# Linear attention and a gated two-layer network: three plain and three large token blocks in place of two and four

## The chip, the cores and the metric

The kernel runs on one core of a Trainium2 chip. TensorE (PE) multiplies 128x128 tiles into PSUM banks; VectorE (DVE), ScalarE (ACT) and GpSimd (POOL) work on tiles in SBUF and PSUM; SyncE (SP) and the other engines issue transfers to and from DRAM. Each engine runs its own instructions in order and waits on semaphores of the others. The metric is the device time of one execution in microseconds (us), and lower is better. Before the change it is 928.02 us, the median of three runs (927.49 to 928.74).

## The reference

There are 8 batches of 576 tokens, with 8 heads of 64. Linear attention is followed by two matrix products with a gate between them:

```python
q_s = softmax(q, axis=-1)            # over the 64 numbers of a head
k_s = softmax(k, axis=2)             # over the 576 tokens of a batch
kv  = einsum('bhsd,bhse->bhde', k_s, v)
x   = einsum('bhsd,bhde->bhse', q_s, kv)   # heads side by side: 4608 x 512
h   = x @ w_in                       # 512 -> 2048
g   = h * clip(h + 3, 0, 6) / 6
out = g @ w_out                      # 2048 -> 512
```

Everything is float32, and the two weight matrices come as 64-bit floats, as raw words.

## The kernel before, in words

**Precision.** A float32 operand is split into a high part `hi` (an ACT cast to fp32r) and a rest `lo` (a DVE subtraction), and each product is three matmuls: hi by hi, hi by lo, lo by hi. `split` (L122 to L124) does that for weights, for x and for g.

**Token blocks.** The 4608 tokens are taken in blocks. The first two are plain blocks of 512. For each of the 16 chunks `f` of 128 hidden numbers, `gemm1` (12 matmuls of 512 columns into a bank `ph`), the gate `relu6` and a split of g into a tile `gp`, then `gemm2` (12 matmuls into four banks `po`). In block 0 a chunk's weights are also decoded from raw words on DVE and ACT (`decode`, L130 to L156, two chunks ahead). Block 0's `gemm2` comes two chunks behind its `gemm1`, block 1's one chunk behind.

The other four are large blocks of 896 tokens. Each product is done by a seven-product scheme on 2x2 blocks (a form of Strassen's), so that seven block products replace eight. `phase1` does the first product of a large block, 56 steps of 6 matmuls of 448 columns, `phase2` the second. The seven combinations of x (`factors`, tiles `right0` to `right6`) and those of g are made on DVE and ACT. The weights' combinations are the same for all large blocks. They are made once and put into two DRAM buffers `kept` (in the profile `wf`), and `fetch` reads them back into tiles `left`, two steps' worth of 512 KB at a time, five groups deep.

**The weights' combinations.** Per pair of chunks and per side (w_in, w_out), three of the seven are plain blocks, written by `plain_weights` from the split weights in SBUF. The other four are sums, made by `sum_weights`: it rebuilds the float32 blocks as hi + lo, with an ACT copy of hi (L430) and an accumulating transfer of lo that POOL issues (L431); then come four DVE passes (L434 to L437), two splits into the chunks' own places, and four transfers to `kept`. Thirteen of the sixteen sums are made in plain block 1. Three (`late_sums`) are made in the first large block's `phase1`, from blocks already in DRAM (L425 and L426, from `kept` and `spare`).

**Attention** is done per pair of heads. For plain blocks it is `attention` (softmax of k and q, nine TensorE transposes, `pkv`, `px`). For large ones it is `sb_attention`: the query softmax `q_softmax_t` runs on transposed tiles, with four POOL copies `swap` for each of its two reductions, a POOL copy `kb` for the k maximum, and a DVE stream transpose into one tile `m`; then come `pm`, `pkv` and `px`. The work is cut into steps, and the loop over chunks advances them: a step or two of the next block's attention per chunk.

**Places.** The decoded weights live in two pools of chunk places (`EARLY`: chunks 0 to 9, then 10 to 15). When the plain blocks are through with a pool, `next_stage` closes it and opens the large blocks' operand tiles there. The PSUM has eight banks, two for attention and six for `ph`, `po` and the large products `x`, `y`, `z`. The ring `v` of three tiles is shared by decode, sums and outputs, `gp` has three.

**What sets the order.** The kernel is written once, and a scheduler that works with planned times sets each engine's order; from plain block 1 on TensorE keeps the program's order. So work written into one block can stand in the one before it, on any of the other engines.

Of the kernel before, what the change touches and what calls it, by code (L numbers as in the profile page):

```python
# [22 lines left out]
TH = 448  # L23
# [9 lines left out]
def attention_moe(  # L33
# [58 lines left out]
    def flip(out, in_):  # L92
# [12 lines left out]
    EARLY = 10  # L105
    stages = [ExitStack(), ExitStack()]
    wp = [
        stage.enter_context(tc.tile_pool(name=f"w{i}", bufs=1, side=side, reuse_waits="tile"))
        for i, (stage, side) in enumerate(zip(stages, ("right", "left")))
    ]  # L110

    def place(f, dt, name):
        return wp[f >= EARLY].tile([P, 4 * DM], dt, name=name, tag=f"w{f}")

# [5 lines left out]
    wi, wo, raws = {}, {}, {}  # L120

# [8 lines left out]
    def decode(f):  # L130
# [17 lines left out]
        nc.vector.tensor_tensor(vu, vu, low, op=ALU.add)  # L148
        parts = place(f, F32R, f"w_{f}").rearrange("p (s i n) -> p s i n", s=2, i=2)
# [39 lines left out]
    def kv_of(j, hp, ke, vt):  # L189
# [9 lines left out]
        kv = att.tile([P, P], F32, name="kv", bufs=8)  # L199
# [50 lines left out]
    def attention(j, hp):  # L250
# [3 lines left out]
        else:  # L254
            kt, ke, vt = load_k(j, hp)
            qt = att.tile([P, TB], F32, name="qt", bufs=2)
# [5 lines left out]
        q_softmax(qt, j == 1, nc.vector if j else nc.gpsimd)  # L262
# [69 lines left out]
    def sb_attention(s, hp):  # L332
        t0 = START + s * SB
        need = [b for b in range(t0 // S, (t0 + SB - 1) // S + 1)]
        qt = att.tile([P, SB], F32, name="qt", bufs=2)
        nc.sync.dma_start(qt, qf[s, hp])
        loads = {b: load_k(b, hp, tokens=True) for b in need if (b, hp) not in kvs}
        new = {}
# [19 lines left out]
        yield  # L358
# [27 lines left out]
    late_sums = [(7, 0), (6, 1), (7, 1)]  # L386
    kept = [dr.tile([P, NSLOT, TB], F32, name=f"wf{i}") for i in range(2)]

    spare = dr.tile([P, len(late_sums), TB], F32, name="spare")

    def keep(pair, side, block, src):
        to = kept[side][:, SLOT[side][pair, PRODUCT[block]]]
        nc.sync.dma_start(to, src)

    def halves(pair, side):

        a, b = (wi, wo)[side][2 * pair], (wi, wo)[side][2 * pair + 1]
        one, two = a[:, :, 0:HT], a[:, :, HT:]
        if side:
            return one, b[:, :, 0:HT], b[:, :, HT:], two  # L400
        return one, two, b[:, :, HT:], b[:, :, 0:HT]

    def plain_weights(pair, side):
        for block, src in zip((A11, A12, A22, None), halves(pair, side)):
            if block is not None:
                to = kept[side][:, SLOT[side][pair, PRODUCT[block]]]
            elif (pair, side) in late_sums:
                to = spare[:, late_sums.index((pair, side))]
            else:
                continue  # L410
# [318 lines left out]
    def steps(units):  # L729
        for unit in units:  # L730
            for _ in unit:
                yield
# [139 lines left out]
```

## Time and profile before

| | |
|---|---|
| median of three runs | 928.02 us (927.49 to 928.74) |
| the profiled execution's own time | 925.28 us |
| its span, first to last instruction | 923.5 us |
| PE busy | 841.9 us (91%), 4328 matmuls |
| DVE busy | 711.8 us (77%) |
| ACT busy | 486.6 us (53%) |
| POOL busy | 141.0 us (15%) |
| DRAM read and written | 174.75 and 39.58 MB |

Busy times are shares of the whole span and average stages that differ: weights are decoded in block 0, sums made in block 1, and only products and attention are left later. In the timeline `x48` after a row means 48 instructions merged into it, and a bracket gives the idle time before the row and what ended it. Most matmuls go through one helper and carry line L87, most splits L123 and L124, so rows are told apart by their tiles.

### The profile page before, as it was taken

Reading aid. Unit: us, or ns where it says so; the run is one execution under the profiler, and the core shown is the slowest. Engines: PE = TensorE matmul, PEld = TensorE weight load, DVE = VectorE, ACT = ScalarE, POOL = GpSimd, SP = SyncE. Lnnn points to the kernel's source line nnn. Section 1 sums busy time; section 2 is a strip of 40 time slices with the busy share of each in tenths; the row PEclk is TensorE's granted clock in tenths of the full one; section 3 lists DMA queues with packets and bytes.
Section 4 is the critical chain, followed back from the end, with each engine's and each line's share of the span. In section 5 each row is a group of like instructions: output and inputs, shape, how many; then the busy total and the mean of one; then the engine's idle time right before and its main releaser. Section 6 shows DMA issues by size and latency. Waiting matters only on the chain.

```text
span 923.5 us, 12980 instructions
## 1 busy us (share of the span) xinstructions
PE 841.9 (91%) x4328; PEld 722.7 (78%) x4328; DVE 711.8 (77%) x1193; ACT 486.6 (53%) x858; POOL 141.0 (15%) x242
## 2 busy tenths in 40 slices
PE   4699986979975888999999999899999999999998
PEld 3478764858763677897898888699889979998997
DVE  7999997478878468989848979984867794555873
ACT  7897642445554345556445555644545644444553
POOL 4112232344543321101101100110100000000000
PEclk9889996999987798999999999999999999999999
DMA  9994545898997896875788887577756668666674
GB/s 371 413 395 162 171 138 163 207 258 231 269 280 245 234 346 222 300 225 178 235 275 287 274 300 227 180 242 253 248 189 188 203 199 265 223 210 206 214 237 154
DMA packets 90291, 222.02 MB, mean 240 GB/s; under 512 B 9072, under 2 KB 35952, under 8 KB 88176
## 3 DMA queue, kind: packets, MB, share of 16 engines
q1 hardware_dynamic: 80432, 211.75, 68.7%
q0 software_dynamic: 9216, 8.39, 5.9%
q10 hardware_dynamic: 576, 1.05, 0.3%
q8 instruction: 35, 0.57, 0.3%
q14 instruction: 32, 0.26, 0.1%
HBM read 174.75 MB, written 39.58 MB: 232 GB/s over the span
## 4 chain that ended last, share of the span: by engine, by line
PE 52%; DVE 23%; issue 9%; DMA 9%; POOL 4%; ACT 2%; SPq 0%; DVEq 0%; ACTq 0%; POOLq 0%
PE x L87 28%; PE y L87 11%; PE z L87 9%; DMA v<-w 3%; POOL v L431 2%; PE px L87 2%; DVE gf L124 2%; DVE v L144 2%; DMA kt<-in_kT_dram 2%; DVE right L124 2%; DVE v L148 2%; DVE g L522 2%; DVE w L124 1%; DMA v<-spare 1%; DVE gp L124 1%
## 5 line engine op out<-in xcount | busy, mean ns | idle before, releaser
L87 PE MATMUL x<-right,left 128*128 128x448 f32 x768 | 178.4, 380 | 16.3 <-DVE g L561 11.7
L123 ACT CAST gf<-g 128x448 fp32r<-128x448 f32 x224 | 126.7, 567 | 125.7 <-PE x L87 57.0
L87 PEld LDWEIGHTS x<-right,left 128*128 128x128 f32 x768 | 146.7, 193 | 33.4 <-DVE g L561 13.0
L87 PE MATMUL x<-gf,left 128*128 128x448 f32 x768 | 163.9, 369 | 4.8 <-DVE gf L124 4.5
L124 DVE TENSOR_TENSOR gf<-g,gf 128x448 fp32r<-128x448 f32 x224 | 135.8, 618 | 38.6 <-ACT gf L123 37.1
L87 PEld LDWEIGHTS x<-gf,left 128*128 128x128 f32 x768 | 144.5, 189 | 20.9 <-DVE gf L124 9.1
L87 PE MATMUL po<-w,gp 128*128 128x512 f32 x384 | 104.4, 422 | 6.4 <-DVE gp L124 3.6
L87 PE MATMUL ph<-x,w 128*128 128x512 f32 x384 | 100.0, 408 | 2.3 <-DVE x L124 1.5
L521 ACT ACTIVATE r<-g,three 128x896 f32<-128x896 f32 (+1 forms) x64 | 54.9, 857 | 83.2 <-DVE g L565 42.2
L87 PEld LDWEIGHTS po<-w,gp 128*128 128x128 f32 x384 | 76.2, 203 | 25.3 <-DVE gp L124 5.1
L87 PEld LDWEIGHTS ph<-x,w 128*128 128x128 f32 x384 | 73.9, 195 | 22.4 <-ACT x L123 2.0
L87 PE MATMUL z<-gf,left 128*128 128x448 f32 x384 | 83.2, 372 | 5.8 <-DVE gf L124 5.5
L87 PE MATMUL y<-right,left 128*128 128x448 f32 x384 | 87.5, 374 | 0.0
L87 PEld LDWEIGHTS z<-gf,left 128*128 128x128 f32 x384 | 72.5, 191 | 15.2 <-DVE gf L124 9.5
L87 PEld LDWEIGHTS y<-right,left 128*128 128x128 f32 x384 | 72.5, 190 | 7.5 <-issue 0.6
L522 DVE SCALAR_TENSOR_TENSOR g<-r,g 128x896 f32<-128x896 f32 (+1 forms) x64 | 54.5, 851 | 9.3 <-ACT r L521 9.3
L431 POOL DMA_DIRECT2D v<-w x52 | 45.7, 1000 | 64.6 <-ACT v L430 28.3
L123 ACT CAST w<-v 128x512 fp32r<-128x512 f32 (+1 forms) x42 | 32.3, 783 | 30.8 <-DVE v L435 21.2
L87 PE MATMUL z<-right,left 128*128 128x448 f32 x192 | 44.8, 368 | 0.0
L304 POOL COPY swap<-qr 32x28 f32<-32x28 f32 x64 | 27.3, 427 | 103.6 <-DVE qr L315 74.8
L565 DVE TENSOR_TENSOR g<-g,y 128x448 f32<-128x448 f32 x32 | 19.7, 617 | 30.1 <-PE y L87 30.1
L87 PE MATMUL px<-m,kv 128*128 128x128 f32 (+6 forms) x112 | 32.3, 436 | 10.8 <-DVE qr L305 10.8
(124 smaller groups left out, 1184.3 us busy)
## 6 DMA issues: line engine op xcount, KB each, us to landing
left<-wf SPq DMA_DIRECT2D x224, 512.0 KB, 4.2
wf<-w SPq DMA_DIRECT2D x100, 256.0 KB, 4.0
raw<-in_w_dram SPq DMA_DIRECT2D x16, 1024.0 KB, 14.0
vt<-in_v_dram SPq DMA_DIRECT2D x28, 325.0 KB, 5.9
kt<-in_kT_dram SPq DMA_DIRECT2D x28, 288.0 KB, 4.9
ke<-in_k_dram SPq DMA_DIRECT2D x24, 320.0 KB, 5.2
qt<-in_qf_dram SPq DMA_DIRECT2D x16, 448.0 KB, 4.2
out_dram<-v SPq DMA_DIRECT2D x16, 448.0 KB, 4.2
```

Of the source, the lines that this page charges most:

```text
L87: nc.tensor.matmul(out, lhsT, rhs, start=start, stop=stop, skip_group_check=goes_on)
L123: nc.scalar.copy(hi, src)
L124: engine.tensor_sub(lo, src, hi.bitcast(F32))
L144: nc.vector.scalar_tensor_tensor(vu, high, 0xC0000000, m, op0=ALU.bitwise_and, op1=ALU.bitwise_or)
L148: nc.vector.tensor_tensor(vu, vu, low, op=ALU.add)
L304: nc.gpsimd.tensor_copy(swap[r : r + QD], stat[o : o + QD])
L431: nc.gpsimd.dma_start(t, src[:, 1].bitcast(F32), accum_op=ALU.add)
L521: nc.scalar.activation(r, h, AF.Relu, bias=three, scale=1.0)
L522: nc.vector.scalar_tensor_tensor(g, r, 6.0, h, op0=ALU.min, op1=ALU.mult)
L565: nc.vector.tensor_add(h21, h21, y)
```

## The change

The block sizes become 3 x 512 and 3 x 1024 tokens. `TH`, half a large block, goes from 448 to 512, so a large product's matmul has 512 columns, and there are three large blocks rather than four. The rest follows:

- Attention for plain block 2 is added (`attention(2, ...)` during block 1), and the first large block's attention is advanced during block 2.
- `decode` also writes the float32 chunk to a DRAM tensor `whole`, for chunks 6 to 15 (`FROM_DRAM = 3` pairs are left out).
- `sum_weights` no longer uses POOL. For the first three pairs it adds hi and lo on DVE (L407), for the others it reads both chunks back from `whole` in one transfer (L410), a step ahead of its use. Its results go to `gp` tiles rather than to the chunks' places. The sixteen sums are spread, a step per chunk, over blocks 1 and 2; none are left for the large blocks.
- There is one pool of chunk places. The `right` tiles use places 0 to 6, the tiles of g places 7 to 14, and of the six `left` groups two use place 15 and four the `gp` ring, which has four tiles. The last plain block takes chunk 15 first.
- `qt` has one buffer rather than two, and an `sb_attention` unit now loads one step before it computes; `px` of a unit comes after the loads of the next. The temporaries of the gate use `g` and `v`.
- The steps that advance the next block's attention and `factors` inside large blocks are at other slots.

```diff
-TH = 448
+TH = 512
...
+    FROM_DRAM = 3
+    whole = dr.tile([P, NFC, 2 * DM], F32, name="whole")
...
+        if f // 2 >= FROM_DRAM:
+            nc.sync.dma_start(whole[:, f], v)
...
-        qt = att.tile([P, SB], F32, name="qt", bufs=2)
+        qt = att.tile([P, SB], F32, name="qt", bufs=1)
         nc.sync.dma_start(qt, qf[s, hp])
         loads = {b: load_k(b, hp, tokens=True) for b in need if (b, hp) not in kvs}
+        yield
...
         w4 = moe.tile([P, 2 * DM], F32, name="v", bufs=3)
-        if late:
-            for n, block in enumerate((A11, A12, A22, None)):
...
-                nc.sync.dma_start(t, src[:, 0:HT])
-                nc.gpsimd.dma_start(t, src[:, HT:], accum_op=ALU.add)
+        if pair < FROM_DRAM:
+            for i in range(2):
+                hi, lo = ((wi, wo)[side][2 * pair + i][:, e].bitcast(F32) for e in (0, 1))
+                nc.vector.tensor_add(w4[:, i * DM : (i + 1) * DM], hi, lo)
         else:
-            for n, src in enumerate(halves(pair, side)):
-                t = w4[:, n * HT : (n + 1) * HT]
-                nc.scalar.copy(t, src[:, 0].bitcast(F32))
-                nc.gpsimd.dma_start(t, src[:, 1].bitcast(F32), accum_op=ALU.add)
+            src = whole[:, 2 * pair : 2 * pair + 2, side * DM : (side + 1) * DM]
+            nc.sync.dma_start(w4.rearrange("p (f n) -> p f n", f=2), src)
+            yield
...
-            if late:
-                dst = moe.tile([P, 2, TB], F32R, name="gp", tag="gp", bufs=3)
-            else:
-                dst = (wi, wo)[side][2 * pair + i]
+            dst = moe.tile([P, 2, TB], F32R, name="gp", bufs=4).rearrange("p i n -> p (i n)")
...
-    GROUP, GROUPS = 2, 5
+    GROUP, GROUPS = 2, 6
...
+    for j in range(NB):
+        if j == 1:
+            in_order.append(True)
+        if j < NB - 1:
+            step = steps([attention(j + 1, hp) for hp in range(NP)], 4)
+        else:
+            step = steps([sb_attention(0, hp) for hp in (0, 2, 1, 3)], 6)
+            fac = factors(0)
+        chunks = [*range(NFC)] if j < NB - 1 else [NFC - 1, *range(NFC - 1)]
+        for n, f in enumerate(chunks):
...
+            if j == 1 and f % 2:
+                plain_weights(f // 2, 0)
+                plain_weights(f // 2, 1)
+            if j:
+                next(sums, None)
...
         def between1(i):
-            if not s and i in (12, 24, 36):
-                sum_weights(*late_sums[i // 12 - 1])
-            if i % 5 in (1, 3):
+            if i % 2:
                 next(step, None)
 
         def between2(i):
-            if i > 16 and i % 2:
+            if i % 2 and i < 16:
                 next(step, None)
-            if i in (31, 33, 35, 37, 39, 41, 43):
+            if i in (18, 21, 33, 36, 39, 42, 45):
                 next(fac, None)
```

How the order of instructions moves is seen at three places. First POOL, in the plain block in which the sums are made. Before, the copies that the large softmax (`swap`) and the k maximum (`kb`) need stand between accumulating transfers:

```order
L304 COPY swap<-qr 32x28 x4
L431 DMA v<-w_309 128x256 x2
L431 DMA v<-w_337 128x256 x2
L431 DMA v<-w_309 128x256
L431 DMA v<-w_337 128x256 x2
L431 DMA v<-w_309 128x256
L431 DMA v<-w_369 128x256 x2
L431 DMA v<-w_425 128x256 x2
L304 COPY swap<-qm 32x28 x2
L343 COPY kb<-km 128x128
```

After the change, from the last split of block 0 on:

```order
L121 TENSOR_TENSOR w_1165<-v,w_1165 128x2x512
L343 COPY kb<-km 128x128
L303 COPY swap<-qm 32x32 x4
L343 COPY kb<-km 128x128
L303 COPY swap<-qr 32x32 x4
L303 COPY swap<-qm 32x32 x4
```

POOL has no transfer left, there or later. Second DVE, at the end of plain block 0, from a chunk's gate (`g<-g,ph`) to the last `kv` that this block's attention makes. Before:

```order
L522 SCALAR_TENSOR_TENSOR g<-g,ph 128x512
L311 TENSOR_REDUCE qm<-qt 128x28
L197 TENSOR_SCALAR rk<-pkv 128x1
L341 TENSOR_REDUCE km<-kt 128x1
L315 TENSOR_REDUCE qr<-qt 128x28
L124 TENSOR_TENSOR gp<-g,gp 128x512
L198 RECIPROCAL rk<-rk 128x1
L200 SCALAR_TENSOR_TENSOR kv<-pkv,rk,mask 128x128
```

After:

```order
L196 TENSOR_SCALAR rk<-pkv 128x1
L121 TENSOR_TENSOR gp<-g,gp 128x512
L219 TENSOR_REDUCE qm<-qt 128x8
L417 TENSOR_TENSOR v<-v 128x256
L197 RECIPROCAL rk<-rk 128x1
L498 SCALAR_TENSOR_TENSOR g<-g,ph 128x512
L419 TENSOR_TENSOR v<-v 128x256
L199 SCALAR_TENSOR_TENSOR kv<-pkv,rk,mask 128x128
```

The passes of the large softmax (`128x28` results) and the large blocks' `km` are gone from here; a plain block's softmax and the first sum (L417, L419) stand in their place. Third DVE again, near the end of the last plain block after the change, where a large block's queries are transposed out of the single `qt` buffer and the next pair's maximum is taken from it:

```order
L320 STREAM_TRANSPOSE m<-qt 128x1024
L121 TENSOR_TENSOR gp<-g,gp 128x512
L498 SCALAR_TENSOR_TENSOR g<-g,ph 128x512
L310 TENSOR_REDUCE qm<-qt 128x32
L121 TENSOR_TENSOR gp<-g,gp 128x512
```

Two rows stand between the transpose and the reduction over the next load of the same buffer. Before the change that reduction read the other buffer.

More of the change, by code (lines that the diff above doesn't have):

```diff
@@ L102, in attention_moe @@
     nc.gpsimd.memset(three, 3.0)
[L105 to L110, printed above, removed]
+    wp = ctx.enter_context(tc.tile_pool(name="wp", bufs=1))
     def place(f, dt, name):
-        return wp[f >= EARLY].tile([P, 4 * DM], dt, name=name, tag=f"w{f}")
+        return wp.tile([P, 4 * DM], dt, name=name, tag=f"w{f}")
     late = iter(range(NFC - 1, -1, -1))
@@ L357, in sb_attention @@
             kv_of(b, hp, ke, vt)
-        yield
         yield
@@ L469, in attention_moe @@
     )
+    turn = iter(range(10**6))
     def fetch(count=1):
@@ L475, in fetch @@
                 return
-            t = operand("left", TB, bufs=GROUPS)
+            at = next(turn) % GROUPS
+            if at > 1:
+                t = moe.tile([P, 2, TB], F32R, name="gp", bufs=4)
+            else:
+                if not ring:
+                    ring.append(place(15, F32R, "left").rearrange("p (r k n) -> p r k n", r=2, k=2))
+                t = ring[0][:, at]
             g = key[2] * GROUP
@@ L727, in attention_moe, with steps @@
     decode(1)
-    def steps(units):
+    def steps(units, length):
+        before = None
         for unit in units:
-            for _ in unit:
+            next(unit)
+            yield
+            if before:
+                next(before, None)
+            for _ in range(length - 2):
+                next(unit)
                 yield
+            before = unit
+        yield
+        next(before, None)
+        yield
     accs = {}
-    done2 = []
     def work(j, n, f, g):
@@ L742, in work, with all_sums @@
             store(j, accs[j])
-        if j and f % 2:
-            plain_weights(f // 2, 1)
-            if (f // 2, 1) not in late_sums:
-                sum_weights(f // 2, 1)
-        if j and f == EARLY - 1:
-            next_stage(0)
-            fetch(GROUPS)
+    def all_sums():
+        for some in (range(FROM_DRAM), range(FROM_DRAM, NPAIR)):
+            for side in range(2):
+                for pair in some:
+                    yield from sum_weights(pair, side)
+    sums = all_sums()
@@ L751, in attention_moe @@
     LAG = 2
     pend = []
-    step = steps([attention(1, hp) for hp in range(NP)])
-    for f in range(NFC):
-        if f + AHEAD < NFC:
-            load_w(f + AHEAD)
-        g = gemm1(0, f)
-        if f + 2 < NFC:
-            decode(f + 2)
-        for _ in range(2 if f % 4 == 3 else 1):
-            next(step, None)
-        pend.append((0, f, f, g))
-        if len(pend) > LAG:
-            work(*pend.pop(0))
-    in_order.append(True)
-    step = steps([sb_attention(0, hp) for hp in (0, 2, 1, 3)])
@@ L782, in attention_moe @@
     for args in pend:
         work(*args)
-    for _ in fac:
+    for _ in sums:
         pass
-    next_stage(1)
+    with tc.high_priority():
+        for _ in fac:
+            pass
+        fetch(GROUPS - 2)
     for s in range(NS):
         more = s + 1 < NS
-        step = steps([sb_attention(s + 1, hp) for hp in (0, 2, 1, 3)]) if more else iter(())
+        step = steps([sb_attention(s + 1, hp) for hp in (0, 2, 1, 3)], 6) if more else iter(())
         fac = factors(s + 1) if more else iter(())
```

104 lines of the change are left out of this document (42 added, 62 removed).

## The prediction

> **What bounds the kernel now.** I read first the table of stages, cut where TensorE changes block, then TensorE's own timeline inside the stages, and last the rows of VectorE (DVE) and GpSimd (POOL) beside each TensorE wait. One row of the stage table is start:end, length, busy time of PE, PEld, DVE, ACT, POOL, then granted clock, DMA share and GB/s.
>
> ```profile
> 0.00:33.70 33.70, 15.51 (x125) 11.25 (x125) 28.16 (x51) 26.64 (x39) 11.31 (x19) 0.90 0.96 384
> 33.70:160.90 127.20, 112.24 (x520) 86.88 (x519) 119.86 (x161) 80.54 (x159) 27.31 (x35) 0.89 0.64 226
> 160.90:289.93 129.03, 111.89 (x584) 88.31 (x584) 96.11 (x185) 67.50 (x133) 60.18 (x90) 0.92 0.92 245
> 289.93:468.90 178.97, 159.96 (x782) 139.52 (x780) 138.88 (x242) 84.71 (x144) 24.56 (x48) 0.93 0.79 253
> 468.90:628.69 159.79, 155.00 (x873) 138.47 (x872) 130.99 (x231) 82.82 (x140) 14.87 (x40) 0.99 0.77 253
> 628.69:780.56 151.87, 149.59 (x781) 132.38 (x780) 109.71 (x182) 78.16 (x132) 2.77 (x10) 1.00 0.69 218
> 780.56:918.94 138.38, 137.60 (x673) 125.86 (x671) 88.11 (x144) 65.22 (x113) 0.00 (x0) 1.00 0.66 213
> 918.94:923.50 4.56, 0.16 (x1) 0.00 (x0) 0.00 (x0) 0.97 (x2) 0.00 (x0) 0.74 0.27 101
> ```
>
> The rows are: the start, plain blocks 0 and 1, large blocks 1 to 4, the tail. (In the timeline, twelve matmuls of block 1 stand ahead of block 0's last 24, so I put their boundary 2.78 us ahead of the group at 163.68.) TensorE is nearly full from 468.9 on; the slack is before that, where clock and PE share are low. How much, the pace tells. TensorE rows are start, length, what ran, and the wait before it:
>
> ```profile
> 72.88 2.96 PE L87 MATMUL ph<-x,w 128*128 128x512 f32 x12
> 75.68 2.92 PE L87 MATMUL po<-w,gp 128*128 128x512 f32 x12
> 78.44 2.96 PE L87 MATMUL ph<-x,w 128*128 128x512 f32 x12
> ...
> 163.68 2.96 PE L87 MATMUL ph<-x,w 128*128 128x512 f32 x12
> ...
> 392.27 9.87 PE L87 MATMUL x<-gf,left 128*128 128x448 f32 x48
> 401.98 9.87 PE L87 MATMUL y<-gf,left 128*128 128x448 f32 x48
> ```
>
> From start to start, 24 matmuls of 512 columns take 5.56 us (0.2317 each) and 48 of 448 take 9.71 us (0.2022 each): time goes with the columns. A plain block has 384 matmuls, 89.0 us; a large one 672, 135.9 us. Attention's share of TensorE, again from start to start:
>
> ```profile
> 84.00 0.71 PE L93 MATMUL pe<-ident,kt 128*128 128x128 f32 x5
> 84.46 3.04 PE L87 MATMUL ph<-x,w 128*128 128x512 f32 x12
> ...
> 90.11 0.60 PE L93 MATMUL tp<-ident,qt 128*128 128x128 f32 x4
> 90.63 0.95 PE L87 MATMUL pkv<-vt,ke 128*64 128x65 f32 x20
> ...
> 100.88 0.91 PE L87 MATMUL px<-qT,kv 128*128 128x448 f32 x2
> ...
> 480.27 1.83 PE L87 MATMUL pkv<-vt,ke 128*64 128x65 f32 x40
> 482.03 2.70 PE L87 MATMUL y<-right,left 128*128 128x448 f32 x12
> ...
> 488.21 1.79 PE L87 MATMUL px<-m,kv 128*128 128x64 f32 x8
> 489.65 2.80 PE L87 MATMUL x<-right,left 128*128 128x448 f32 x12
> ```
>
> One head pair of a plain block costs 0.46 + 0.52 + 0.88 (half of 1.76) + 0.9 = 2.76 us; of a large block with two new batches 1.76 + 1.44 = 3.20, with one 0.88 + 1.44 = 2.32. There are four pairs per block. So floor and loss of each stage are: block 0, 89.0 + 11.0 = 100.0, loss 27.2; block 1, 89.0 + 12.8 = 101.8, loss 27.2; large 1, 135.9 + 9.3 = 145.2, loss 33.8; large 2, 148.7, loss 11.1; large 3, 145.2, loss 6.7; large 4, 135.9, loss 2.5. With start and tail the floors make 815, the losses 108.5.
>
> Where do they come from?
>
> ```profile
> 135.94 1.08 PE L93 MATMUL tp<-ident,qt 128*128 128x128 f32 x4 [2.49 <-DVE x L124]
> 150.38 1.86 PE L87 MATMUL px<-qT,kv 128*128 128x448 f32 x2 [6.50 <-DVE kv L200]
> 156.53 7.32 PE L87 MATMUL po<-w,gp 128*128 128x512 f32 x24
> ...
> 140.94 1.09 DVE L311 TENSOR_REDUCE qm<-qt 128x28 f32<-128x896 f32 x1 [2.08 <-DMA qt<-in_qf_dram]
> ...
> 204.76 0.42 DVE L434 TENSOR_TENSOR v<-v 128x256 f32<-128x256 f32 x1 [4.77 <-DMA v<-w]
> ...
> 205.93 3.33 PE L87 MATMUL px<-m,kv 128*128 128x128 f32 x8 [5.86 <-DVE qr L305]
> 208.80 4.14 PE L87 MATMUL po<-w,gp 128*128 128x512 f32 x12
> ...
> 303.74 2.69 POOL L426 DMA_DIRECT2D v<-wf  x3 [14.94 <-DMA v<-wf]
> ...
> 309.55 0.75 DVE L341 TENSOR_REDUCE km<-kt 128x1 f32<-128x576 f32 x1 [6.50 <-POOL kb L343]
> ...
> 310.88 4.85 PE L87 MATMUL x<-right,left 128*128 128x448 f32 x12 [4.49 <-DVE g L561]
> ```
>
> At 140.9 DVE is inside the first large block's query softmax while block 0 still runs; `kv` stands behind it and TensorE waits 6.50. At 204.8 DVE stands 4.77 us in front of an accumulating transfer, `kv` behind it, TensorE 5.86. From 288.8 to 303.7 POOL waits for such a transfer, `kb` stands behind it and its three successors, DVE waits 6.50 for `kb`, and the drain of the product banks queues behind DVE. A wait costs more than itself: after the 5.86 us the eight `px` took 3.33 (1.79 usually) and the next twelve `po` 4.14 (2.92), 2.8 us more. The Trainium skill, TensorE: Matmul & The Clock Gate, "What's actually happening", has the clock halved after an idle window of about 3.4 us until as much time busy; this trace agrees there.
>
> **The change part by part.**
>
> *TensorE work.* 1152 plain matmuls instead of 768 and 2016 large instead of 2688, these now of 512 columns: 1152 x 0.2317 + 2016 x 0.2022 x 8/7 = 266.9 + 465.9 = 732.8 against 177.9 + 543.5 = 721.4, +11.4 us. The Trainium skill's spacing (same page, "Wait — 56ns, not 53.3ns?": N/2.4 + 2.5 ns warm) would make it +9.4; the trace's 231.7 and 202.2 ns are above its 215.8 and 189.2, so the trace is used. Attention: four more plain pairs, +11.0; large blocks with 2, 2 and 1 new batches and `px` 8/7 as long (1.65): 4 x (3.41 + 3.41 + 2.53) = 37.4 against 4 x (3.20 + 2.32 + 3.20 + 2.32) = 44.2, -6.8. Floors after: start 33.7, blocks 100.0, 100.0, 102.6, large 168.9, 165.4, 155.3, tail 4.6: 830.5, that is +15.4. The change buys this with losses.
>
> *Block 0.* Two rows price what is added here and below, a 512-wide pass on DVE and the landing of a 512 KB transfer:
>
> ```profile
> L124 DVE TENSOR_TENSOR gp<-g,gp 128x512 fp32r<-128x512 f32 x32 | 21.7, 679 | 1.4 <-ACT gp L123 1.4
> left<-wf SPq DMA_DIRECT2D x224, 512.0 KB, 4.2
> ```
>
> The large softmax leaves its end, and the second attention takes its place on DVE (per pair two reductions and one 512-wide multiply rather than five 896-wide passes). Gone are the waits of 2.49 and 6.50, and with them the slow groups behind (24 `po` in 7.32 for 5.56, and the like): I take 12 of 27.2 off and leave 15. Added are ten 512 KB copies of decoded chunks to DRAM on SP's queue. They hold a `v` buffer until landed; of three, one is reused three chunks later, some 16 us at 5.56 each, against 4.2 us of landing, and the DMA share is 0.64. So I cost them at nothing; if a copy were held behind a `kt` load that waits for its buffer, DVE would stop in the next decode. Bounds 13 (all waits and slow groups gone) to 27.2.
>
> *The sums.* 64 accumulating transfers on POOL and 52 ACT copies go. Sums of the first three pairs add hi and lo on DVE: 12 passes of about 0.68 us, in block 1 where DVE was busy 96 of 129. The others read 512 KB a step ahead on SP, so DVE waits only if that transfer is more than a chunk late. Eleven sums' worth of DVE work is in block 1, five in block 2, instead of thirteen in block 1 and three in large 1. With POOL's queue holding only `swap` and `kb`, the rows at 204.76 and 309.55 have no cause left. Block 1: loss 6 (the first three chunks carry three sums together, more than DVE clears at TensorE's pace); bounds 2.5, the loss of the undisturbed last large block, to 27.2. Block 2: it holds two-batch attention, five sums and the split of the first operands, bunched in its last third; loss 10 with the hand-over, bounds 2.5 to 27.2.
>
> *Large 1.* Today's hand-over and late sums:
>
> ```profile
> 292.06 0.60 ACT L702 ACTIVATE v<-po 128x512 f32<-128x512 f32 x1 [3.40 <-DVE w L124]
> ...
> 297.13 2.61 PE L87 MATMUL x<-right,left 128*128 128x448 f32 x6 [4.59 <-ACT g L552]
> ...
> 591.00 4.65 PE L87 MATMUL z<-gf,left 128*128 128x448 f32 x20 [1.67 <-DVE gf L124]
> ```
>
> ACT's drain of block 1 waited for a `v` buffer that a sum held, the copy of the first product stood behind it, TensorE waited 4.59. After, no sum is left there. What remains resembles large 2 (also two new batches): DVE 131.0 of a floor of 148.7 is 0.88, and 131.0 x 8/7 of 168.9 is 0.89. So loss 11; bounds 6.7 to 33.8. Operands now stand in weights' places and in `gp`: the first `left` groups reuse chunk 15, run first for that, the rest follow the last `gp`; six groups of 512 KB at 2.8 us each cover the 4.2 us of landing, as five of 2.4 do now. Nothing added.
>
> *Large 2 and 3* answer to today's 3 and 4, with the next operands' splits moved to slots with less DVE work (591.00 is such a wait): losses 7 and 3; bounds 2.5 to 11.1 and 2.5 to 6.7.
>
> **Sum**: 830.5 + 15 + 6 + 10 + 11 + 7 + 3 = 882.5 us of span, against 923.5. The profiled execution's own time was 925.28, 1.78 above its span, and the median of the runs 928.02, 2.74 above that: 882.5 + 4.5 = **887 us**. All lower bounds give 830.5 + 30 + 4.5 = 865; all upper ones 830.5 + 133 + 4.5 = 968.
>
> **The rivals.**
>
> *One query buffer (slower).* `qt` goes from two buffers to one, so a pair's queries load only after the pair before is transposed.
>
> ```profile
> L311 DVE TENSOR_REDUCE qm<-qt 128x28 f32<-128x896 f32 x16 | 17.3, 1081 | 8.4 <-DMA qt<-in_qf_dram 8.4
> qt<-in_qf_dram SPq DMA_DIRECT2D x16, 448.0 KB, 4.2
> ```
>
> With two buffers DVE already stood 8.4 us in all before this reduction; a load takes 4.2. In the new order at the end of block 2 two rows (1.35 us) stand between transpose and next reduction, and the `gp` that TensorE needs stands behind it. If each of the 11 later large pairs puts 4.2 us and the 2.8 of slow clock on TensorE, that is 77 us: 964. It decides from (928 - 887) / 11 = 3.7 us a pair. For it: DVE runs in order. Against: elsewhere five or more rows lie between, and `px` comes four steps later.
>
> *DVE stays the bound of the sums' blocks.* Blocks 1 and 2 lose 27.2 each as block 1 does now: 887 + 21 + 17 = 925. For it: the DVE bunches named above. Against: the waits I found there stand before transfers and POOL, not before DVE work.
>
> *Almost no long wait left.* Losses near the bounds, 865 to 870. For it: large 4 loses 2.5 and the waits named are gone. By the Trainium skill's window of 3.4 us (same page and section as above) the waits I left, 1 to 3 us each, would slow nothing behind them; no row here settles how short a wait is free.
>
> *The change doesn't do what it says*: excluded but for a scheduler that puts the large softmax back into block 0; the order shows block 0 free of it.
>
> **How the numbers follow.** Forecast (870 to 905) 0.60; almost no wait 0.15; DVE bound (905 to 935) 0.13; one buffer (above 935) 0.10; nothing 0.02. The range 864 to 924 takes in the first two and half of the third. A measurement tells 0.2% from no change, about 1.9 us: faster 0.84, same 0.03, slower 0.13.
>
> **What would show it.** Right: POOL without DMA rows; no TensorE wait above 3 us between about 60 us and the first large block; block 0 ending near 149, large 1 beginning near 367, large blocks of some 180, 172 and 158. Wrong: `qm<-qt` idle on its load above 30 us in all (one buffer); blocks 1 or 2 above 120 us with waits on `gp` (DVE); decode waiting for DRAM copies (block 0); `left` groups late in the large blocks.

## The result and the profile after

The changed kernel takes 871.38 us, the median of four runs (867.29 to 873.27), against 927.75 us (922.49 to 928.74) of the kernel before on the same chip: a ratio of 0.9397, 95% interval 0.9348 to 0.9446. It is faster by 56 us where 41 were forecast. Its profiled execution took 867.29 us, the lowest of the four, and its span is 865.5 us.

The stages of the kernel after, in the columns of the prediction's first table: the start, three plain blocks, three large ones, the tail.

```profile
0.00:33.53 33.53, 16.69 (x124) 12.41 (x125) 28.15 (x51) 26.73 (x39) 11.30 (x19) 0.89 0.96 384
33.53:148.24 114.71, 106.78 (x519) 83.96 (x517) 105.94 (x140) 81.73 (x172) 17.91 (x7) 0.96 0.72 263
148.24:253.34 105.10, 100.47 (x517) 80.81 (x516) 78.98 (x157) 51.16 (x123) 4.75 (x18) 1.00 0.59 203
253.34:364.80 111.46, 106.05 (x586) 85.02 (x584) 88.68 (x152) 48.99 (x73) 12.64 (x40) 0.98 0.56 194
364.80:539.12 174.32, 170.98 (x873) 136.75 (x872) 147.18 (x232) 90.19 (x139) 16.02 (x40) 1.00 0.71 238
539.12:706.97 167.85, 166.15 (x782) 132.67 (x780) 127.22 (x190) 87.26 (x134) 5.56 (x18) 1.00 0.62 203
706.97:860.43 153.46, 152.61 (x673) 125.90 (x671) 97.91 (x144) 72.00 (x113) 0.00 (x0) 1.00 0.58 189
860.43:865.50 5.07, 0.17 (x1) 0.00 (x0) 0.00 (x0) 1.06 (x2) 0.00 (x0) 1.00 0.28 103
```

TensorE is at full clock from 53.6 us on, early in block 0, but for one stretch of 3.4 us in block 2. The span and the mean granted clock of the kernel before, and then of the kernel after:

```profile
core 0: 923.5 us, clock 0.954
```

```profile
core 0: 865.5 us, clock 0.988
```

A mean of 0.954 means 84 us of the span at half speed, as the clock records of the trace add up, one of 0.988 means 20 us. So up to 32 of the 58 us of span that went, half of the 64, are TensorE running slowly after waits; the waits themselves and the pace make the rest.

What TensorE still waits for (the wait, us in all, how often, the longest), without the waits of the start:

```profile
PE po L87 <- DVE gp L121: 4.3, 2, 2.2
PE x L87 <- DVE g L538: 3.6, 3, 1.9
PE tp L93 <- ACT ke L246: 3.1, 2, 2.4
...
PE pe L93 <- ACT ke L246: 2.4, 3, 1.0
```

None of the waits of 4.5 to 6.5 us of before is left. And the pace, in the timeline of block 0 and of the last large block:

```profile
71.49 2.88 PE L87 MATMUL ph<-x,w 128*128 128x512 f32 x12
74.21 2.88 PE L87 MATMUL po<-w,gp 128*128 128x512 f32 x12
76.93 2.88 PE L87 MATMUL ph<-x,w 128*128 128x512 f32 x12
...
827.80 5.60 PE L87 MATMUL x<-gf,left 128*128 128x512 f32 x24
833.24 5.60 PE L87 MATMUL x<-gf,gp 128*128 128x512 f32 x24
```

From start to start twelve matmuls take 2.72 us and 24 take 5.44: 0.2267 us each, in both blocks, where the prediction had 0.2317 in plain and 0.2311 in large blocks. The sum can be redone with that one number: a plain block's matmuls 87.05 us rather than 89.0, a large block's 152.3 rather than 155.3.

| stage | forecast | measured | loss forecast | loss at the measured pace |
|---|---|---|---|---|
| block 0 | 115.0 | 114.7 | 15 | 16.7 |
| block 1 | 106.0 | 105.1 | 6 | 7.1 |
| block 2 | 112.6 | 111.5 | 10 | 10.8 |
| large 1 | 179.9 | 174.3 | 11 | 8.4 |
| large 2 | 172.4 | 167.9 | 7 | 5.4 |
| large 3 | 158.3 | 153.5 | 3 | 1.2 |

The losses add up to 49.6 us against 52 forecast. The 17 us of span by which the forecast was too long are 15 us of pace and 2 of losses.

### The profile page after: what moved, and what is told of

Same layout as the page of the kernel before. It is cut to its first block, busy times and chain, and to the rows that moved or that the text cites. A ratio compares the mean times of both kernels' runs of the same rounds, so it can differ in the third digit from the quotient of the medians.

```text
span 865.5 us, 11820 instructions
## 1 busy us (share of the span) xinstructions
PE 819.9 (95%) x4064; PEld 657.5 (76%) x4064; DVE 674.1 (78%) x1064; ACT 459.1 (53%) x789; POOL 68.2 (8%) x142
## 4 chain that ended last, share of the span: by engine, by line
PE 60%; DVE 16%; DMA 5%; issue 4%; ACT 3%; POOL 1%; ACTq 0%; DVEq 0%; SPq 0%; POOLq 0%
PE x L87 25%; PE y L87 10%; PE z L87 9%; PE po L87 7%; PE ph L87 6%; DVE g L498 2%; DVE gp L121 1%; DMA kt<-in_kT_dram 1%; PE px L87 1%; DMA wf<-gp 1%; PE pkv L87 1%; ACT qt L221 1%; DMA out_dram<-v 1%; DMA v<-whole 1%; POOL swap L303 1%
## 5 line engine op out<-in xcount | busy, mean ns | idle before, releaser
L120 ACT CAST gf<-g 128x512 fp32r<-128x512 f32 x168 | 104.2, 624 | 96.4 <-DVE gf L121 48.6
L121 DVE TENSOR_TENSOR gf<-g,gf 128x512 fp32r<-128x512 f32 x168 | 113.3, 689 | 31.7 <-ACT gf L120 31.0
L87 PEld LDWEIGHTS po<-w,gp 128*128 128x128 f32 x576 | 107.3, 190 | 30.2 <-DVE gp L121 5.4
L87 PE MATMUL x<-right,gp 128*128 128x512 f32 x384 | 95.0, 392 | 2.8 <-DVE g L538 2.8
L87 PE MATMUL x<-gf,gp 128*128 128x512 f32 x384 | 89.0, 389 | 0.0
L87 PEld LDWEIGHTS x<-right,gp 128*128 128x128 f32 x384 | 71.6, 188 | 19.1 <-DVE g L538 3.6
L87 PEld LDWEIGHTS x<-gf,gp 128*128 128x128 f32 x384 | 72.1, 188 | 15.0
L87 PE MATMUL x<-right,left 128*128 128x512 f32 x192 | 47.8, 392 | 0.8 <-DVE g L538 0.8
L87 PE MATMUL y<-right,gp 128*128 128x512 f32 x192 | 48.2, 395 | 0.0
L498 DVE SCALAR_TENSOR_TENSOR g<-g,ph 128x512 f32<-128x512 f32 x48 | 32.4, 677 | 15.4 <-ACT g L497 15.3
L87 PEld LDWEIGHTS x<-gf,left 128*128 128x128 f32 x192 | 35.7, 188 | 9.7 <-DVE gf L121 2.5
L87 PEld LDWEIGHTS x<-right,left 128*128 128x128 f32 x192 | 35.7, 188 | 8.6 <-DVE g L538 1.3
```

The costliest lines, as they stand in the source:

```text
L87: nc.tensor.matmul(out, lhsT, rhs, start=start, stop=stop, skip_group_check=goes_on)
L120: nc.scalar.copy(hi, src)
L121: engine.tensor_sub(lo, src, hi.bitcast(F32))
L498: nc.vector.scalar_tensor_tensor(g, r, 6.0, h, op0=ALU.min, op1=ALU.mult)
```

## The experiments

Two things are to be found out: which part of the change gave the 56 us, and where the pace came from. Times are compared by their ratio to the kernel before on the same chip; the changed kernel's is 0.9397.

**The sums back on GpSimd.** In the changed kernel, every sum again copies hi by ACT and adds lo by an accumulating transfer on GpSimd's queue; no float32 copies in DRAM.

```
-    hi and lo added on DVE (pairs 0 to 2), or whole[...] read back
+    nc.scalar.copy(t, hi[:, k_ * HT : (k_ + 1) * HT])
+    nc.gpsimd.dma_start(t, lo[:, k_ * HT : (k_ + 1) * HT], accum_op=ALU.add)
```

> The changed kernel, but every sum again rebuilds its float32 blocks with ACT copies and accumulating transfers issued by POOL, as before the change, and no float32 copies go to DRAM; block sizes, places and the step at which each sum is made stay. Theory (the losses of plain block 1 and large block 1 came from POOL's transfers and from DVE standing before them): before, thirteen such sums went with a loss of 27 us in one block; sixteen spread over two blocks should put 12 to 25 us back, 883 to 896 us, with DVE waits on v<-w of some 20 us in all and TensorE waits of 3 to 6 us at px. Rival (the block sizes and the spreading alone made the gain): within 3 us of the changed kernel's 871.

Measured: 889.02 us (885.11 to 889.53), ratio 0.9594 (0.9536 to 0.9651), as the theory had it. Its block 1 by the stage table, and the largest waits of DVE in that stretch:

```profile
149.82:270.20 120.38, 108.02 (x517) 84.61 (x516) 75.11 (x145) 62.33 (x162) 41.82 (x58) 0.94 0.75 196
```

```profile
DVE v L412 <- DMA v<-w: 8.1, 7, 1.8
...
DVE v L414 <- DMA v<-w: 3.8, 2, 3.0
```

Block 1 is 15.3 us longer than the changed kernel's 105.1 and DVE does less in it (75.1 us for 79.0): it stands in front of the transfers. Block 2 is 3.1 longer, the large blocks 1.8. The details of the theory came out in part: DVE waits 15.1 us in all for `v<-w` where some 20 were expected, and the waits of TensorE in block 1 stand ahead of the key transposes (the longest 3.5 us), none ahead of `px`. The edit takes the copies in DRAM away too; against the kernel that lacks only these (867.87 us, below) it is 21 us.

**The kernel before with its sums on DVE.** The other way round: before's order and blocks, only that hi and lo are added on DVE (the three late sums load both parts first).

```
-    nc.scalar.copy(t, src[:, 0].bitcast(F32))
-    nc.gpsimd.dma_start(t, src[:, 1].bitcast(F32), accum_op=ALU.add)
+    nc.vector.tensor_add(t, src[:, 0].bitcast(F32), src[:, 1].bitcast(F32))
```

> The kernel before with the sums' hi + lo made by a DVE addition in place of an ACT copy and an accumulating POOL transfer (the three late sums load both parts into a tile and add); block sizes and the place of the sums in the program stay. Theory: POOL's queue is free, block 1 loses 12 to 18 instead of 27 (DVE has 22 us more to do) and large block 1 some 15 instead of 34: 893 to 905 us. Rival (the waits belong to the number of sums in block 1, whoever adds): within 5 us of the kernel before.

Measured: 904.98 us (904.04 to 907.3), ratio 0.9783 (0.9736 to 0.983), some 20 us below before, at the upper end of what the theory gave. Its block 1:

```profile
161.18:276.74 115.56, 107.77 (x584) 85.52 (x584) 110.33 (x239) 51.71 (x84) 14.34 (x34) 0.96 0.66 226
```

It takes 115.6 us instead of 129.0, with more work on DVE (110.3 us for 96.1): over the floor of 101.8 it loses 13.8 us, as the theory had it. From the first large block on it is only 6.6 us shorter, where the theory took 19 off that block alone. So the transfers, with the ACT copies that go with them, are worth some 18 to 21 us whichever kernel they are put into.

**Two plain blocks and four large.** The changed kernel, its sums, places and single query buffer, with before's blocks: `TH` = 448, two steps of the sums for each chunk.

```
-TH = 512
+TH = 448
...
+                next(sums, None)
...
-_OUTS = [((1536, 512), "float32"), ((3, 512, SB), "float32")]
+_OUTS = [((1024, 512), "float32"), ((4, 512, SB), "float32")]
```

> The changed kernel's sums, places and order, but two plain blocks of 512 and four large ones of 896 as before; the sums are advanced two steps per chunk so that they end in plain block 1. Theory: TensorE's floor is about 811 us, some 14 less than with three and three, but block 1 must now hold sixteen sums (16 x 3 us of DVE), the large softmax and the first split, about 130 us of DVE against a floor of 100, so it loses some 30 us: 878 to 900 us, slower than the changed kernel. Rival 1 (only the way the sums are made matters, and DVE has room for them): 860 to 868, faster than the changed kernel. Rival 2 (the block sizes made the gain): 915 or more.

Measured: 888.18 us (882.55 to 888.66), ratio 0.9584 (0.9532 to 0.9636): 17 us of the gain hang on the block sizes, with them the third plain block. Its block 1:

```profile
152.40:281.80 129.40, 111.65 (x586) 86.75 (x585) 117.89 (x225) 59.05 (x93) 20.64 (x48) 0.93 0.79 277
```

All sixteen sums and the softmax of a large block fall into one plain block there, and DVE is busy 91% of it. In the changed kernel the same work lies in two blocks, in which DVE is busy 75 and 80%.

**One query buffer.** The kernel before with one buffer for the queries instead of two: the rival of the prediction that was to make the kernel slower, tried alone.

```
-            qt = att.tile([P, SB], F32, name="qt", bufs=2)
+            qt = att.tile([P, SB], F32, name="qt", bufs=1)
```

(and the same for the plain blocks' `qt`).

> The kernel before with one qt buffer in place of two, nothing else. Theory: the wait for the query load is hidden or spread, within 6 us of the kernel before. Rival (one query buffer, 3.7 us or more for each of some 15 large pairs): 40 us or more slower.

Measured: 908.45 us (907.86 to 910.06), ratio 0.982 (0.9774 to 0.9865): 17 us faster, which neither theory had. The large blocks' query reductions of the kernel before (shortest, median and longest ns, first and last start in us), and then of this one:

```profile
L311 DVE TENSOR_REDUCE qm<-qt x16: 1074/1078/1087, 118.6 to 654.4; 128x28 f32<-128x896 f32 x16
```

```profile
L311 DVE TENSOR_REDUCE qm<-qt x16: 1071/1085/1087, 139.6 to 658.5; 128x28 f32<-128x896 f32 x16
```

With two buffers the softmax of the first large block begins at 118.6 us, in the middle of block 0, and parts of three pairs' softmax stand on DVE ahead of `kv`. With one it cannot begin before the plain queries are gone, at 139.6. Block 0 ends 10.6 us earlier:

```profile
33.90:150.28 116.38, 109.79 (x520) 86.07 (x519) 108.31 (x140) 80.11 (x157) 22.21 (x19) 0.93 0.66 235
```

That is 116.4 us where the change has 114.7: what the prediction took off block 0 because its next block is plain, one buffer gives without that. The changed kernel with two query buffers was not run. Block 1 is 4.7 us shorter as well (124.3). The wait for the load of the queries, the price that was feared, is 4.5 us in all on DVE in the changed kernel (8.4 before).

**Both in the kernel before.** One query buffer and the sums on DVE, both edits as above.

> The kernel before with two of the change's parts together: one query buffer instead of two (908.5 us alone, 17.1 below the kernel before on the same chip) and the sums' hi and lo added on VectorE (905.0 alone, 20.5 below); two plain and four large blocks, the pools and places of before. Theory: the two act at different places, the large softmax at the end of block 0 and the transfers of block 1 and the first large block, so they add: 925.5 - 17.1 - 20.5 = 888, that is 884 to 893 us, which is where two plain and four large blocks with all the rest of the change stood (888.2); then operands in the weights' places, float32 copies and addresses have given next to nothing there, and three plain and three large blocks the 17 us that are left. Rival: the two take the same waits away, or VectorE becomes the bound of block 1 once both are gone: 895 to 905 us, and the rest of the change has given some 10 us more.

Measured: 894.19 us (893.52 to 899.1), ratio 0.9678 (0.9614 to 0.9743), 29.5 us below before: between what theory and rival gave. The spans went down by 17.3 and 19.8 us apart and go down by 31.8 together, so some 5 us of the two gains are lost; the ratios have 7 us, which their intervals do not show clear of noise. Its block 1, and the largest wait in it:

```profile
149.90:275.10 125.20, 110.16 (x585) 87.39 (x584) 120.70 (x255) 54.72 (x86) 16.95 (x39) 0.93 0.64 220
```

```profile
248.18 3.33 PE L87 MATMUL px<-m,kv 128*128 128x128 f32 x8 [7.96 <-DVE m L321]
```

DVE is busy 120.7 of 125.2 us. The softmax that one buffer moved out of block 0 meets the sums in block 1, and TensorE waits 8 us for the queries behind both. This is the rival in which DVE bounds the sums' block. It is real with two plain blocks, and the third plain block is what removes it.

**No copies in DRAM.** The changed kernel with all sums added on DVE.

```
-    whole = dr.tile([P, NFC, 2 * DM], F32, name="whole")
...
-            nc.sync.dma_start(whole[:, f], v)
...
-            nc.sync.dma_start(w4.rearrange("p (f n) -> p f n", f=2), src)
+            nc.vector.tensor_add(w4[:, i * DM : (i + 1) * DM], hi, lo)
```

> The changed kernel without the float32 copies in DRAM: all 16 sums add hi and lo on VectorE, at the same points of the program; ten 512 KB copies and ten 512 KB loads go. The prediction costed the copies at nothing in block 0. Theory: that holds, block 0 stays at 114.7 us within 1 us, and the ten sums that now add instead of load cost VectorE 20 passes of about 0.64 us, 12.8 us, in blocks 1 and 2, where it is busy 79 of 105 and 89 of 111 us; a part of it shows: 871 to 880 us. Rival: the copies slow the decode or the loads of block 0, which then becomes shorter by more than 2 us, and the run is faster than the changed kernel: 864 to 869 us.

Measured: 867.87 us (865.65 to 869.75), ratio 0.9372 (0.9323 to 0.9421), which cannot be told from the changed kernel. Block 0 has the length that the theory gave, and no part of the added work shows in the time, which lies in the rival's range. Blocks 0, 1 and 2:

```profile
33.50:148.69 115.19, 108.94 (x519) 85.76 (x518) 106.38 (x141) 81.62 (x172) 17.93 (x7) 0.92 0.60 217
148.69:252.70 104.01, 100.40 (x517) 80.77 (x516) 85.77 (x167) 51.20 (x122) 5.49 (x18) 1.00 0.50 175
252.70:362.63 109.93, 105.13 (x586) 83.68 (x584) 93.05 (x160) 49.20 (x73) 12.37 (x40) 1.00 0.53 178
```

Block 0 is no shorter without ten copies. But it is not the same block 0 otherwise: the order on TensorE has changed at its end. The last head pair's `pkv`, its `px` and the block's last `po`, in the changed kernel and then in this one:

```profile
129.09 0.95 PE L87 MATMUL pkv<-vt,ke 128*64 128x65 f32 x20
...
142.52 0.92 PE L87 MATMUL px<-qT,kv 128*128 128x448 f32 x2
...
145.50 5.61 PE L87 MATMUL po<-w,gp 128*128 128x512 f32 x24
```

```profile
137.33 0.95 PE L87 MATMUL pkv<-vt,ke 128*64 128x65 f32 x20
...
140.44 1.86 PE L87 MATMUL px<-qT,kv 128*128 128x448 f32 x2 [1.79 <-DVE kv L196]
...
144.72 6.85 PE L87 MATMUL po<-w,gp 128*128 128x512 f32 x24
```

Without copies 3 us lie between `pkv` and `px` rather than 13, TensorE waits for `kv`, and the clock is at half speed from 140.4 us for 6.9 us. The wait and half of that time make up to 5 us, and block 0 is only 0.5 us longer. So this run does not show that the copies cost block 0 nothing: something else in it is shorter by about as much, and whether that is the copies is open. DVE takes 11 us more work in blocks 1 and 2 without either becoming longer: there the copies buy nothing.

**The pace: fewer columns.** The changed kernel with 384 of 512 columns in the large products.

```
+                    st = n in (0, 1, 2) and not c and not m
+                    u = TH if st else COLS
-                    mm(to, w_[:, cs], f_[:, c], ...)
+                    mm(to[:, 0:u], w_[:, cs], f_[:, c, 0:u], ...)
```

> The changed kernel, with every matmul of the large blocks' Strassen products cut from 512 to 384 columns, but for the first one into each bank (1920 of 2016 matmuls); 128 of 512 columns of those products are left out. It settles the pace term, the one that the changed kernel's trace shows off: 512 columns measured 0.2267 us from start to start where 0.2311 was taken, by scaling the 448-column 0.2022 with the columns. Theory: at 448 columns something that does not go with the columns, such as the weight load of 188 ns that each matmul has, set the 0.2022; then 384 columns do not go below it much: 24 matmuls in the last large block take 4.5 to 4.9 us from start to start (0.188 to 0.202 each), and the whole run 820 to 850 us. Rival: time goes with the columns, as the prediction took it: 24 matmuls in 4.1 us (0.170), and the run below 815 us unless VectorE, busy 147 of the first large block's 174 us, becomes the bound there.

Measured: 805.12 us, one run. In its last large block:

```profile
760.79 4.32 PE L88 MATMUL x<-gf,left 128*128 128x384 f32 x24
764.95 8.61 PE L88 MATMUL z<-gf,gp 128*128 128x512 f32 x48
```

24 matmuls take 4.16 us, 0.1733 each, below the 0.188 of a weight load. The theory falls: the weight load sets no floor here, at 448 columns least of all. The rival comes close, with 0.170 and a run below 815 us. From 384 to 512 columns it is 0.0533 us for 128, so 0.417 ns a column, and 13.3 ns that every matmul has. By this line 448 columns would take 0.2000.

**The pace: 64 bytes.** Sorting the matmuls of both traces by the tiles' addresses in the built programs gave another theory.

```
+    pad = wp.tile([P, 16], F32, name="pad")
+    nc.gpsimd.memset(pad, 0.0)
```

> The changed kernel with 64 bytes reserved ahead of the sixteen weight places, so that the weights, and the large blocks' operands that take their places, lie 64 bytes further in each partition; x, gp and gf stay, and the program is the same otherwise. Both kernels' traces show that a matmul of 512 columns takes 213.3 ns and 13.3 more, mostly, where the moving data and the weights both start 32 bytes behind a multiple of 128; in the kernel before, ten of sixteen weight chunks start 96 bytes behind one, and with x moving against them not one in a hundred of the matmuls is that fast (19.7 ns more on average), with gp loaded against them a quarter (16.6). Theory: the place in SBUF sets the pace. Then 12 ph in a row take 2.79 to 2.81 us rather than 2.72 from start to start, po 2.74 to 2.78; summed over 576 ph (5.6 ns), 576 po (2.5), 1008 of phase 1 (2.5 to 4) and the third of 1008 in phase 2 that loads the ring's places (5.6), 9.5 us: 878 to 884 us. Rival: the pace belongs to something else of the two kernels (transfers, the length of the rows): 2.72 us for 12 stays, 869 to 873 us.

Measured: 874.66 us (871.47 to 878.67), ratio 0.9476 (0.944 to 0.9511). The timeline of its block 0:

```profile
70.16 2.96 PE L87 MATMUL ph<-x,w 128*128 128x512 f32 x12
72.96 2.92 PE L87 MATMUL po<-w,gp 128*128 128x512 f32 x12
75.72 2.96 PE L87 MATMUL ph<-x,w 128*128 128x512 f32 x12
```

`ph` takes 2.80 us and `po` 2.76 where both took 2.72, as the theory had it, and the kernel before shows the same 2.80 and 2.76 in its rows from 72.88. All matmuls of 512 columns with another straight behind (under 245 ns from start to start), sorted by the byte in a line of 128 at which their moving data and the weights of the one behind start:

```
kernel      moving  weights  matmuls  mean ns  up to 227 ns
after       32      32       2982     227.4    85%
before      32      32        239     228.9    55%
before      32      96        208     233.0     1%
before      96      32        198     229.9    26%
before      96      96         12     231.3    17%
64 bytes    32      32        681     227.8    70%
64 bytes    32      96        817     233.1     2%
64 bytes    96      32       1133     229.7    27%
64 bytes    96      96        361     228.1    64%
```

What counts at 512 columns is not where the weights lie but whether moving data and weights lie alike: 96 with 96 is fast again. (The twelve of the kernel before are all `po` between two tiles `w`; the 42 such matmuls of the 64-byte kernel are as slow, 230.7 ns, against 228.1 for its whole row.) At 448 columns it is the other way round: in the kernel before, 1277 matmuls with moving data at 32 and weights at 96 take 202.3 ns, 1243 with both at 96 take 204.8. The mean over the four rows of this kernel is 230.0 ns, which for 3168 matmuls is 8 us more than at 227.4; the theory's 9.5 had 96 with 96 as slow. 4.2 us are seen in the span (869.7); 2 were won by less time at half clock (16.2 us for 20.5), the others lay where TensorE had to wait anyway or were not found. The pace at 512 columns is settled by this. The median stays below what the theory gave; by the ratios the run is 7 us slower than the changed kernel, and the two intervals just touch.

**Can it be made faster?** Three edits to the changed kernel. First, a plain pair's query transposes one step behind its key transposes:

```
         next(ks, None)
+        yield
         tp = (bank_a if j else bank)("tp")
...
-            step = steps([attention(j + 1, hp) for hp in range(NP)], 4)
+            step = steps([attention(j + 1, hp) for hp in range(NP)], 5)
```

> The changed kernel with the query transposes of a plain attention pair one step behind its key transposes rather than in the same step, so that ScalarE has a chunk's time to copy the key banks. In the changed kernel TensorE waits for those copies 3.1 us in front of the query transposes and 2.4 us in front of the key transposes. Theory: these waits go, nothing takes their place, 865 to 870 us. Rival: they are covered by, or move to, the waits for VectorE's operands: 870 to 874 us.

Measured: 862.28 us (861.02 to 863.93), ratio 0.9314 (0.9267 to 0.9361). Block 1 goes from 105.1 to 102.1 us and block 0 from 114.7 to 111.9; the profiled span is 3.4 us shorter (862.1), the medians are 9 apart; the profiled execution is the lowest of the changed kernel's and the highest of this one's. The waits ahead of the query transposes are gone, as the theory had it. Ahead of the key transposes three of 0.7 us are left, and a wait of 2.04 us for `gp` at 137.16 us in the changed kernel, which the theory did not name, is gone from block 0. Second, activation and split of a plain chunk's operand ahead of other ready work:

```
-        relu6(g, g, ph)
-        split(gp[:, 0], gp[:, 1], g)
+        with tc.high_priority():
+            relu6(g, g, ph)
+            split(gp[:, 0], gp[:, 1], g)
```

> The changed kernel with the activation and the split of a plain chunk's second operand put ahead of other ready work in the order on VectorE and ScalarE. The changed kernel's TensorE waits for that operand (gp) 4.3 us behind VectorE, once behind the first large operands in block 2 (2.2 us, with the next twelve matmuls in 4.4 instead of 2.9 us). Theory: the bunch in block 2 is what costs, block 2 becomes 2 to 4 us shorter, 866 to 870 us. Rival: what is put back by it (kv, the decode of block 0, the next block's softmax) becomes late and costs as much or more: 871 to 885 us.

Measured: 866.23 us (865.08 to 867.95), ratio 0.9351 (0.9296 to 0.9406). The time is that of the theory, its reason is not: block 2 stays at 111.3 us, with a wait of 2.21 us for `gp` still in it, and the gain is in block 0 (111.4), where the wait of 2.04 us is gone here too. Block 1 is 2.2 us longer (107.3), with 3.4 us at half speed. Both together:

> Two edits together that gave something apart: the query transposes one step behind the key transposes (862.3 alone), and activation and split of a plain chunk's second operand ahead of other ready work (866.2 alone). Theory: they remove different waits, ScalarE's copies of the key banks and VectorE's bunch behind the large operands, so most of both gains adds up: 856 to 860 us. Rival: both take the same clock-halving waits away, 861 to 865 us.

Measured: 862.49 us (861.31 to 864.76), ratio 0.9342 (0.9315 to 0.9369): no more than the first alone. Both shorten the same block 0 (112.1 here), by the same wait. Both and no copies in DRAM:

> The same two edits and no float32 copies in DRAM (all sums add hi and lo on VectorE; 867.9 alone). Theory: with VectorE's order fixed, the 12.8 us of further passes find room in blocks 1 and 2, and the loads that go are off the path: 852 to 858 us, faster than with the two edits alone. Rival: VectorE, busy 79 of 105 and 89 of 111 us there already, comes late with the operands: slower than the two edits alone by 2 to 6 us.

Measured: 869.04 us (867.41 to 874.08), ratio 0.9424 (0.9392 to 0.9456), 6.5 us slower than with the copies. The time is the rival's, again not its reason: blocks 1 and 2 take 213.1 us together against 213.7, with the added work hidden as before. It is block 0, where only the first sum begins, that has become longer, 117.1 us against 112.1, at a lower clock. Block 0 of this kernel, and then of the one with both edits:

```profile
33.80:150.91 117.11, 109.86 (x519) 86.28 (x518) 105.35 (x141) 81.51 (x172) 18.37 (x7) 0.91 0.60 214
```

```profile
34.20:146.25 112.05, 106.92 (x518) 84.52 (x517) 105.12 (x140) 81.42 (x173) 18.12 (x7) 0.95 0.73 267
```

It is the end of block 0 that was seen without copies above: 3.6 us lie between the last `pkv` and its `px` rather than 8.7, TensorE waits 2.25 us for `kv`, and the clock is at half speed from 140.3 us for 10.3 us, where the kernel with both edits has none. The kernel with the sums back on GpSimd, which lacks the copies too, has the same order, a wait of 1.56 us and 6.8 us at half speed there. Why leaving out ten transfers changes that order is open. The fastest version is the first edit, alone or with the second, some 5 to 8 us below the changed kernel by the ratios; the intervals still touch.

## Why the prediction was right, and where its sum was wrong

*Block 0* (loss 15 forecast, 16.7 measured): the mechanism holds, as one query buffer alone shows with block 0 at 116.4 us. That the copies cost nothing there is not shown: the run without them has another order at the end of block 0.

*The sums* (losses 6 and 10 forecast, 7.1 and 10.8 measured): the transfers on GpSimd's queue were the cause, put back they cost 17.6 us, and of the 21.7 us between the two spans 15.3 are in block 1. GpSimd has no DMA rows any more, and no wait of TensorE between 60 us and the first large block is above 2.22 us. The bunch of large operands at the end of block 2 is there: DVE makes them from 329 to 344 us, and this is the one place behind block 0 where the clock drops.

*The large blocks* (11, 7 and 3 forecast, 8.4, 5.4 and 1.2 measured): a little better in each. Why was not taken apart.

*The step that failed* is the first term of the sum, "1152 x 0.2317 + 2016 x 0.2022 x 8/7", +11.4 us. With the means of the table and of the 448-column matmuls of before (203.5 ns over 2519 of them) it was 768 x 0.2305 + 2688 x 0.2035 = 724.0 us and became 3168 x 0.2274 = 720.4: 3.6 us less, not 11.4 more. Two things were mis-sized. The 0.2317 of the plain blocks was taken over as a property of 512 columns, while it was one of weights that lay 64 bytes off the data; the change laid all operands alike. And the 0.2022 of 448 columns was scaled by 8/7 with its fixed share: "time goes with the columns" was read from two numbers that were both off the line for different reasons, and the reason of the second, 448 columns, is open. With 15 us less the forecast would have been 872; this term is why 871 lies at the lower end of 870 to 905.

*The rivals.* One query buffer does not make the kernel slower; in the kernel before it was worth 17 us by itself, and the prediction did not see that it was a cause of its own gain. DVE as the bound of the sums' blocks is refuted for the changed kernel (79 of 105 and 89 of 111 us) and shown for two plain blocks (118 of 129 and 121 of 125). "Almost no long wait left" comes near the time, 865 to 870, for another reason: the losses are those of the forecast, not the bounds.

So of the 56 us some 30 come from one query buffer and the sums on DVE, which in the kernel before get into each other's way in block 1; the block sizes, whose third plain block gives the sums a second block, give 17 more. The rest, 6 to 9 us between 894 and 888 by times or ratios (the two intervals overlap), would lie in the places, copies and addresses, and was not taken apart.

## What to carry to other kernels

A second buffer can cost time: it lets the work of a later stage start early and stand, on an engine that runs in order, ahead of what the present stage waits for, so look at when the first instruction of each stage begins. When two edits each remove a wait of the same engine, try them together before adding their gains, since one may move its work to where the other has put its own. A duration per matmul is only carried to another shape or layout once a second row has told the fixed part from the part that goes with the columns, and once it is known whether the operands lie alike in SBUF.

## What was not expected of the hardware

A matmul of 512 columns with a fresh weight load takes 226.7 ns in long undisturbed rows, 13.3 above 0.417 ns a column by the line through 384 and 512 columns; where moving data and weights start 64 bytes apart in a line of 128, it takes 233.1 (moving at 32, weights at 96) or 229.7 (the other way round) on average. The Trainium skill, TensorE: Matmul & The Clock Gate, "Wait — 56ns, not 53.3ns?", has N/2.4 + 2.5 ns, 215.8 for 512 columns. The slope agrees with the 0.417 ns measured here; the fixed part, here with a fresh weight load for each matmul, is larger.

448 columns stay above the line however the operands lie: 203.7 ns on average in the kernel with two plain and four large blocks, where all lie alike, and in the kernel before 204.8 where they lie alike and 202.3 where they do not; the line gives 200.0. So lying alike is faster at 512 columns and not at 448. Why was not found out.

A wait shorter than 3.4 us costs too. In the kernel after:

```profile
342.84 1.37 PE L87 MATMUL po<-w,gp 128*128 128x512 f32 x4 [2.22 <-DVE gp L121]
344.00 4.37 PE L87 MATMUL ph<-x,w 128*128 128x512 f32 x12
348.21 2.91 PE L87 MATMUL po<-w,gp 128*128 128x512 f32 x12
```

After a wait of 2.22 us twelve matmuls take 4.21 us for 2.72, 1.5 us more; the clock records have half speed from 343.7 to 347.1. The Trainium skill, same page, "What's actually happening", has the clock go down after at least one idle window of about 3.4 us. This trace has it go down after 2.22 us of waiting, so the reading in the prediction's rival "Almost no long wait left", that waits of 1 to 3 us slow nothing behind them, is not safe.

The length of the wait alone does not decide: the wait of 2.04 us that ended at 137.16 was followed by no drop. The clock records of all traces change in steps of 3.41 us. Behind 60 us the fourteen traces together have 3148 such steps at full speed in which the matmul rows fill over 54% of the time, and none is followed by half speed; of 46 in which they fill less than 44%, every one is; of the 25 between, twelve are. The step before 343.7 us is filled to 35%. The wait of 2.04 us fell into two steps, the second of them filled to 51%.
